# Pooling of batches 1 to 3 in column tiles, its exponentials turned by transposing DMAs, side jobs grouped next to phases, input loads paced by a GpSimd copy

## The chip, the cores and the metric

The kernel runs on one core of a Trainium2 chip. Its engines are PE (TensorE: matmuls; PEld is its weight load), DVE (VectorE), ACT (ScalarE), POOL (GpSimd) and SP (SyncE, which here only issues DMAs). The metric is device microseconds (us) of one execution, as a median over runs; less is better.

## The reference

Four batches of 12544 tokens with 128 features, 32 inducing vectors:

```python
def mab(q, kv):
    s = scale * (q @ kv.transpose(0, 2, 1))
    s = s - s.max(-1, keepdims=True)
    a = np.exp(s)
    a /= a.sum(-1, keepdims=True) + 1e-09
    return a @ kv
h = mab(I, x)          # pooling: 32 vectors h from 12544 tokens
y = mab(x, h)          # every token attends to the 32 vectors
g = np.maximum(y @ w1, y @ w2)
out = g @ w_out        # d_ff = 1024, result f32
```

## The kernel before, in words

A batch is cut into 98 chunks of 128 tokens; there are 392 chunks. The kernel rewrites max(y w1, y w2) w_out as relu(y (w2 - w1)) w_out plus a linear part y w1 w_out, and folds h into the weights: `hwd` = h (w2 - w1) and `m1` = h w1 w_out, so that y itself is never formed.

For each batch there are two parts.

- Pooling. The tokens of a batch arrive as seven loads (`load_x`, L160, issued by POOL) into tiles `xn` (14 chunks each), of which there are 12. SP turns them into `xT` with 14 transposing DMAs (`transpose_x_dma`, L164). For each of the seven parts, `p1_scores` (L244) makes 14 matmuls with a chunk of `xT` as weights (128x128) and the 32 inducing vectors as moving operand, and ACT takes the exponential into `et` (tokens on partitions). `p1_accum` (L262) makes 14 more matmuls with a chunk of `xn` as weights and the 32 columns of `et` as moving operand; the sum stays in PSUM for a part, then DVE adds it to `hacc` (L303). POOL adds up the exponentials themselves in `eacc` (L305), folds them (`small_fold`, L308), and `small_h` sums them over partitions with four f32 matmuls against ones (L339), takes the reciprocal and scales. `small_hwd` and `small_m1` make the folded weights. Batch 0 is pooled before the main loop, in another way; batches 1 to 3 are pooled in the main loop, between the output work of the batch before.
- Output. `stage` (L464) makes the second exponentials `e2` for a block of up to 16 chunks: four matmuls in column tiles (128 rows by 32 columns of the PE array, all four side by side, L479), then one exponential. A `phase` (L771) is up to four jobs in row tiles (32 rows by 128 columns, L827), one per PSUM bank: hidden units of `hwd` for one quarter, or the linear part. A relu of 128x512 on ACT (L843) or DVE (L846) takes each bank to SBUF. `final_one` (L652) is a full-array matmul of 128x128x128, eight per chunk, 3136 in all; when a group of up to four chunks is complete, DVE scales it by the softmax denominator (`evict_group`, L692) into one of six tiles `o` and SP stores it (L717).

The order of instructions on every engine is written by the program itself when it is built: an object `Clock` keeps an estimated time for PE, ACT, DVE and each of the eight PSUM banks, and the loop at L909 picks the next piece of PE work from it. A change of tiling mode (full array, row tiles, column tiles) is charged in that estimate. Pooling jobs are put on a list `jobs_at` by the number of finished output chunks (L859 to L876); `side_work` (L880) takes the first pending job if its inputs are ready by the estimate and the PE is in full-array mode. The estimate knows nothing of SP's queue: a transposed part counts as usable a fixed time after its issue.

Of the kernel before, what the change touches and what calls it, by code (L numbers as in the profile page):

```python
# [16 lines left out]
INF = 1e9  # L17
# [85 lines left out]
def kernel(  # L103
# [53 lines left out]
            xn_at[b, i] = xn_tiles[nslot % NXN]  # L157
            nslot += 1

    def load_x(b, i):  # L160
        k0, n = parts[b][i]
        nc.gpsimd.dma_start(out=xn_at[b, i][:, 0:n, :], in_=xr[b, :, k0 : k0 + n, :])  # L162

    def transpose_x_dma(b, j):  # L164
# [23 lines left out]
    inducingT = consts.tile([C, M], F16, name="inducingT")  # L188
    m1bd = consts.tile([128, 4, C], F16, name="m1bd")
    rep32 = consts.tile([128, 128], F32, name="rep32")  # L190
    diag = consts.tile([128, M], F32, name="diag")

    with tc.manual_schedule(engines={ET.PE, ET.DVE, ET.Activation, ET.Pool, ET.SP}):
        nc.sync.dma_start(ind_sb, inducing)
# [16 lines left out]
        for q in range(4):  # L211
# [1 line left out]
        nc.gpsimd.memset(m1bd, 0.0)  # L213

        nc.vector.reduce_sum(out=diag, in_=identity32.rearrange("p (k m) -> p m k", m=M), axis=AX.X)
        nc.vector.tensor_scalar(
            out=rep32.rearrange("p (k m) -> p k m", m=M),
            in0=diag[:, None, :].broadcast_to((128, 4, M)),
            scalar1=DOWN / scale,
            scalar2=None,  # L220
            op0=ALU.mult,
        )

        st = [dict() for _ in range(B)]

# [36 lines left out]
        def p1_accum(b, i):  # L262
            k0, n = parts[b][i]
            et, ready = st[b].pop(("et", i))
            xn = xn_at[b, i]
            if b == 0:
                last = i == len(parts[0]) - 1
                ck.wait(ready, "p1")
                for j in range(n):
                    nc.tensor.matmul(  # L270
                        out=st[0]["hps"][:, 0:M],
                        lhsT=xn[:, j, :],
                        rhs=et[:, j, :],
                        start=(i == 0 and j == 0),
                        stop=(last and j == n - 1),
                    )
                for j in range(0, n, 4):
                    m = min(4, n - j)
                    nc.tensor.matmul(
                        out=st[0]["eps"][0 : m * M, 0:1],  # L280
                        lhsT=et[:, j : j + m, :].rearrange("p k m -> p (k m)"),
                        rhs=ones16[:, 0:1],
                        start=(i == 0 and j == 0),
                        stop=(last and j + m >= n),
                        skip_group_check=True,
                    )
                st[0]["end"] = ck.run(0.029 * n + 0.03 * ((n + 3) // 4))
                return
            bi, ps = bank([128, 512])
            ck.wait(max(ready, ck.bank[bi]), "p1")  # L290
            for j in range(n):
                nc.tensor.matmul(  # L292
                    out=ps[:, 0:M], lhsT=xn[:, j, :], rhs=et[:, j, :], start=(j == 0), stop=(j == n - 1)
                )
            end = ck.run(0.029 * n)
            if i == 0:
                st[b]["hacc"] = smp.tile([C, M], F32, name=f"hacc_{b}", tag="hacc")
                nc.vector.tensor_copy(out=st[b]["hacc"], in_=ps[:, 0:M])
                st[b]["eacc"] = smp.tile([128, P1, M], F32, name=f"eacc_{b}", tag="eacc")
                nc.gpsimd.tensor_copy(out=st[b]["eacc"], in_=et)  # L300
            else:
                acc = st[b]["hacc"]
                nc.vector.tensor_add(out=acc, in0=ps[:, 0:M], in1=acc)  # L303
                acc = st[b]["eacc"]
                nc.gpsimd.tensor_add(out=acc, in0=acc, in1=et)  # L305
            ck.bank[bi] = ck.on_dve(end, 0.1)

        def small_fold(b):  # L308
            e = st[b]["eacc"]
            nc.gpsimd.tensor_add(out=e[:, 0:7, :], in0=e[:, 0:7, :], in1=e[:, 7:14, :])  # L310
            nc.gpsimd.tensor_add(out=e[:, 0:3, :], in0=e[:, 0:3, :], in1=e[:, 3:6, :])

        def small_h(b):
            hT4 = smp.tile([C, 4, M], F16, name=f"hT4_{b}", tag="hT4")
            if b == 0:


                nc.vector.tensor_scalar(
                    out=hT4,
                    in0=st[0]["hps"][:, None, 0:M].broadcast_to((C, 4, M)),  # L320
                    scalar1=DOWN,
                    scalar2=None,
                    op0=ALU.mult,
                )
                st[b]["hT4r"] = ck.on_dve(st[0]["end"], 0.3)
                ck.bank[st[0]["hb"]] = st[b]["hT4r"]
                es = smp.tile([128, 1], F32, name="es_0", tag="es")
                nc.scalar.copy(out=es, in_=st[0]["eps"][:, 0:1])
                ready = ck.on_act(st[0]["end"], 0.2)
                st[b]["hT4"] = hT4.rearrange("c q m -> c (q m)")  # L330
                return es, ready
            rec = smp.tile([C, M], F32, name=f"hrec_{b}", tag="hrec")
            if True:
                bi, ps = bank([128, 512])
                e = st[b]["eacc"]
                use = [0, 1, 2, 6]
                ck.wait(ck.bank[bi], "p1")
                for n, i in enumerate(use):
                    nc.tensor.matmul(  # L339
                        out=ps[:, 0:M], lhsT=ones32, rhs=e[:, i, :], start=(n == 0), stop=(n == len(use) - 1)  # L340
                    )
                end = ck.run(0.11 * len(use))
                nc.vector.reciprocal(out=rec, in_=ps[:, 0:M])
                ck.bank[bi] = ck.on_dve(end, 0.35)
                hsrc = st[b]["hacc"]
            nc.vector.tensor_mul(
                hT4,
                hsrc[:, None, :].broadcast_to((C, 4, M)),
                rec[:, None, :].broadcast_to((C, 4, M)),
            )  # L350
            st[b]["hT4r"] = ck.on_dve(0.0, 0.25)
            st[b]["hT4"] = hT4.rearrange("c q m -> c (q m)")

        def small_sums(es, ready):
# [239 lines left out]
        state = {"g": 0, "mm": 0, "lin": 0, "done": 0, "issued": 0}  # L594
        ptr = [[0, 0] for _ in range(4)]
        chunks_done = [0]

        def unit_src(g, chunk, jb):
            q, t = chunk
# [82 lines left out]
        def evict_group(g, end):  # L682
# [33 lines left out]
            for b, c, s, m in runs:  # L716
                nc.sync.dma_start(out=outr[b, :, c : c + m, :], in_=osb[:, s : s + m, :])  # L717
            chunks_done[0] += n

        def finals_left():  # L720

# [28 lines left out]
            return g  # L750

        LINEAR_AHEAD = 18
        MARGIN = 0
        LIMIT = -16

        def plan_phase(linear=True):
# [93 lines left out]
                ptr[q][1] += 1  # L850
                state["issued"] += 1

        jobs_at = {}
        DONE0 = [0, 98, 196, 294]

        def at(n, f, *a):
            jobs_at.setdefault(n, []).append((f, a))

        for b in range(1, B):  # L859
            base = DONE0[b - 1]  # L860
            p_first, p_step = (16, 5) if b == 1 else (0, 7)
            t_first, t_step = (8, 2.2) if b == 1 else (-14, 3.4)
            for i in range(7):
                s = int(p_first + p_step * i)
                at(base + s, p1_scores, b, i)
                at(base + s + 2, p1_accum, b, i)
            end = base + int(p_first + p_step * 6)
            at(end + 2, small_fold, b)
            at(end + 4, small_h, b)
            at(end + 5, small_hwd, b)  # L870
            at(end + 6, small_m1, b)
            for j in range(14):
                at(base + int(t_first + t_step * j), transpose_x_dma, b, j)
            if b > 1:
                for i in range(7):
                    at(base - 34 + 3 * i, load_x, b, i)  # L876

        pending = []

        def side_work():  # L880
            while jobs_at and min(jobs_at) <= chunks_done[0]:
                pending.extend(jobs_at.pop(min(jobs_at)))
            while pending:
                f, a = pending[0]
                if f in (p1_scores, p1_accum, small_h, small_hwd, small_m1):
                    if min(ck.bank) > ck.pe + 0.1 or ck.mode != "full":
                        return
                    if f is p1_scores and st[a[0]]["T", 2 * a[1] + 1] + 6.0 > ck.pe:
                        return
                    if f is p1_accum and st[a[0]]["et", a[1]][1] > ck.pe:  # L890
                        return
                    if f is small_m1 and a[0] == 0 and w_of["w1out"] > ck.pe:
                        return
                    if f in (small_hwd, small_m1) and st[a[0]]["hT4r"] > ck.pe:
                        return
                    pending.pop(0)
                    f(*a)
                    return
                pending.pop(0)
                f(*a)  # L900

        phase(plan_phase(False))
        phase(plan_phase(False))
        stage(blocks[1])
        weights_3()
        pending.append((small_m1, (0,)))
        nstage = 2
        START = ck.pe
        while state["g"] < len(groups):  # L909
            side_work()  # L910
            need = [ptr[q][0] for q in range(4)]
            if nstage < len(blocks):
                left = []
                for q in range(4):
                    next_job(q)
                    k, u = ptr[q]
                    left.append(sum(len(blk.units[q]) for blk in blocks[k:nstage] if q < len(blk.units)) - u)
                free = nstage < NE2 or min(g.blk.index for g in groups[state["g"] :]) > nstage - NE2
                if min(left) <= 3 and free and min(ck.bank) <= ck.pe + 0.1 and all(
                    "hT4" in st[qu.b] and "hwd" in st[qu.b] for qu in blocks[nstage].quarters if qu  # L920
                ):
                    stage(blocks[nstage])
                    nstage += 1
                    continue
            jobs = plan_phase()
            tp = INF
            tf = final_ready()
            useful = len(jobs) == 4 or jobs and (tf >= INF or nstage == len(blocks) and lag() <= 48)
            if useful and len(jobs) > 0:
                fr = sorted(ck.bank)[len(jobs) - 1]  # L930
                tp = max([fr - 0.095] + [(a.blk.staged if kind == "L" else a.staged) for kind, q, a, u in jobs])
            if tp < INF and lag() <= 128 + LIMIT and (tp <= ck.pe - MARGIN or tp <= tf and tf > ck.pe):
                phase(jobs)
            elif tf < INF:
                keep_busy(tf)
# [40 lines left out]
```

## Time and profile before

| what | value |
|---|---|
| median of 13 runs | 340.91 us (338.96 to 343.48) |
| the profiled execution | 339.68 us |
| its span | 337.9 us |
| DMA | 50.60 MB, mean 150 GB/s |
| POOL adds of exponentials (L305) | 18 of 1034 ns |
| issue of an input load on POOL (L162) | 550 ns |

The span is the part of the execution between its first and last traced instruction; 1.8 us lie around it. Busy times are unions of the instructions' own intervals, and matmuls overlap their neighbours, so PE's work is better read from the distance between the starts of groups in the timeline than from the length of a matmul: a matmul of 128 columns lasts 220 ns, yet its successor starts 56 ns later.

### The profile page before, as it was taken

Reading aid. Unit: us, or ns where it says so; the run is one execution under the profiler, and the core shown is the slowest. Engines: PE = TensorE matmul, PEld = TensorE weight load, DVE = VectorE, ACT = ScalarE, POOL = GpSimd, SP = SyncE. Lnnn points to the kernel's source line nnn. Section 1 sums busy time; section 2 is a strip of 40 time slices with the busy share of each in tenths; the row PEclk is TensorE's granted clock in tenths of the full one; section 3 lists DMA queues with packets and bytes.
Section 4 is the critical chain, followed back from the end, with each engine's and each line's share of the span. In section 5 each row is a group of like instructions: output and inputs, shape, how many; then the busy total and the mean of one; then the engine's idle time right before and its main releaser. Section 6 shows DMA issues by size and latency. Waiting matters only on the chain.

```text
span 337.9 us, 13042 instructions
## 1 busy us (share of the span) xinstructions
PE 328.9 (97%) x5636; PEld 255.3 (76%) x5636; DVE 286.8 (85%) x525; ACT 279.4 (83%) x532; POOL 45.5 (13%) x72
## 2 busy tenths in 40 slices
PE   7888999999999999999999999999999999999996
PEld 3776767777777777787777778877777777777786
DVE  2248989989988899998899989889999998898873
ACT  2559888986996998888998888887989899989961
POOL 7270002234000012134000012121000000000000
PEclk9999999999999999999999999999999999999999
DMA  7999889938985769529975679631222321231233
GB/s 129 212 263 213 190 205 188 198 109 166 242 228 152 177 146 187 137 95 175 249 212 139 145 165 199 130 99 66 101 89 95 111 95 72 90 124 67 95 126 111
DMA packets 60313, 50.60 MB, mean 150 GB/s; under 512 B 42304, under 2 KB 44768, under 8 KB 60256
## 3 DMA queue, kind: packets, MB, share of 16 engines
q1 hardware_dynamic: 54576, 35.35, 39.6%
q0 software_dynamic: 5680, 14.42, 22.0%
q8 instruction: 44, 0.72, 0.8%
q14 instruction: 13, 0.11, 0.1%
HBM read 27.80 MB, written 25.69 MB: 158 GB/s over the span
## 4 chain that ended last, share of the span: by engine, by line
PE 85%; POOL 1%; ACT 1%; DMA 1%; DVE 1%; issue 1%; SPq 1%; POOLq 0%
PE ps L652 56%; PE ps L827 21%; PE ps L479 2%; PE ps L249 2%; PE ps L292 2%; PE ps L339 1%; DMA xT<-xn 1%; PE ps L519 1%; POOL eacc L305 1%; DVE relu L846 1%; ACT relu L843 1%; POOL eacc L310 0%; SPq L168 0%; PE ps L371 0%; PE ps L630 0%
## 5 line engine op out<-in xcount | busy, mean ns | idle before, releaser
L843 ACT ACTIVATE relu<-ps 128x512 f16<-128x512 f32 x460 | 245.8, 600 | 38.3 <-PE ps L827 32.0
L846 DVE TENSOR_SCALAR relu<-ps 128x512 f16<-128x512 f32 x324 | 208.7, 681 | 21.1 <-PE ps L827 19.0
L652 PE MATMUL ps<-woutp,relu 128*128 128x128 f16 x3136 | 222.3, 220 | 0.0
L652 PEld LDWEIGHTS <-relu 128*128 128x128 f16 x3136 | 177.3, 98 | 38.4 <-issue 27.8
L827 PE MATMUL ps<-e,hwd 32*128 32x512 f16 (+2 forms) x880 | 88.7, 360 | 0.4 <-ACT e L491 0.3
L692 DVE TENSOR_TENSOR o<-ps,rp 128x512 f32<-128x512 f32 (+3 forms) x108 | 68.5, 634 | 8.3 <-PE ps L652 5.4
L827 PEld LDWEIGHTS <-hwd 32*128 32x128 f16 x880 | 24.9, 91 | 20.8 <-issue 1.1
L827 PE MATMUL ps<-m,e 32*128 32x128 f16 x381 | 38.6, 217 | 0.0
L305 POOL TENSOR_TENSOR eacc<-eacc,et 128x448 f32<-128x448 f32 x18 | 18.6, 1034 | 82.1 <-ACT et L258 82.1
L827 PEld LDWEIGHTS <-e 32*128 32x128 f16 x381 | 21.3, 93 | 2.9 <-issue 0.2
L258 ACT ACTIVATE et<-ps 128x448 f16<-128x448 f32 (+2 forms) x29 | 15.6, 538 | 3.1 <-PE ps L249 3.0
L249 PE MATMUL ps<-inducingT,xT 128*128 128x32 f16 x392 | 15.5, 177 | 1.6 <-DMA xT<-xn 0.8
L162 POOL DMA_DIRECT2D xn<-in_x_dram x29 | 15.7, 550 | 2.3 <-POOLq L960 0.8
L249 PEld LDWEIGHTS <-xT 128*128 128x128 f16 x392 | 13.1, 96 | 2.5 <-DMA xT<-xn 1.0
L300 POOL CAST eacc<-et 128x448 f32<-128x448 f16 x3 | 1.7, 556 | 89.9 <-ACT et L258 89.9
L237 DVE COPY xT<-ps 128x1024 f16<-128x1024 f16 (+2 forms) x8 | 5.1, 633 | 9.6 <-PE ps L233 9.6
L240 ACT COPY xT<-ps 128x768 f16<-128x768 f16 (+2 forms) x8 | 5.6, 704 | 8.8 <-PE ps L233 8.8
L491 ACT ACTIVATE e<-ps 128x512 f16<-128x512 f32 (+2 forms) x21 | 11.9, 571 | 0.0
L479 PE MATMUL ps<-xT,hT 128*32 128x512 f16 (+3 forms) x114 | 10.5, 367 | 0.1
L292 PE MATMUL ps<-et,xn 128*128 128x32 f16 x294 | 10.6, 176 | 0.0
L292 PEld LDWEIGHTS <-xn 128*128 128x128 f16 x294 | 9.7, 96 | 0.0
L233 PE MATMUL ps<-identity,xn 128*128 128x128 f16 x98 | 6.8, 220 | 0.7 <-DMA xn<-in_x_dram 0.7
(75 smaller groups left out, 99.8 us busy)
## 6 DMA issues: line engine op xcount, KB each, us to landing
out_dram<-o SPq DMA_DIRECT2D x90, 256.0 KB, 2.4
xn<-in_x_dram POOLq DMA_DIRECT2D x27, 448.0 KB, 11.7
out_dram<-o SPq DMA_DIRECT2D x10, 128.0 KB, 2.1
wf<-in_moe_w_dram POOLq DMA_DIRECT2D x4, 256.0 KB, 12.1
xT<-xn SPq DMA_TRANSPOSE x42, 3.4
out_dram<-o SPq DMA_DIRECT2D x6, 64.0 KB, 1.8
out_dram<-o SPq DMA_DIRECT2D x2, 192.0 KB, 3.3
xn<-in_x_dram POOLq DMA_DIRECT2D x1, 256.0 KB, 13.7
```

The lines of the kernel that those rows point to most:

```text
L162: nc.gpsimd.dma_start(out=xn_at[b, i][:, 0:n, :], in_=xr[b, :, k0 : k0 + n, :])
L249: nc.tensor.matmul(out=ps[:, j * M : (j + 1) * M], lhsT=xT_tiles[b % 2][:, k0 + j, :], rhs=inducingT, start=True, stop=True,)
L258: nc.scalar.activation(out=et[:, 0:n, :], in_=ps[:, 0 : n * M], func=AF.Exp, scale=scale)
L292: nc.tensor.matmul(out=ps[:, 0:M], lhsT=xn[:, j, :], rhs=et[:, j, :], start=(j == 0), stop=(j == n - 1))
L305: nc.gpsimd.tensor_add(out=acc, in0=acc, in1=et)
L479: nc.tensor.matmul(out=ps[32 * q : 32 * (q + 1), 128 * t : 128 * (t + n)], lhsT=hq, rhs=xT[:, c : c + n, :], start=True, stop=True, tile_p ...
L491: nc.scalar.activation(out=blk.e2[:, 0 : 128 * wd], in_=ps[:, 0 : 128 * wd], func=AF.Exp, scale=st[0]["rs"] if blk.b == 0 else scale,)
L652: nc.tensor.matmul(out=g.ps[:, 128 * c : 128 * (c + 1)], lhsT=g.blk.relu[q][:, 128 * (jb * w4 + t) : 128 * (jb * w4 + t + 1)], rhs=woutp[: ...
L692: nc.vector.tensor_mul(osb[:, 0:n, :], g.ps[:, 0 : n * C].rearrange("p (s c) -> p s c", s=n), rp)
L827: nc.tensor.matmul(**seq[i])
L843: nc.scalar.activation(out=dst, in_=src, func=AF.Relu)
L846: nc.vector.tensor_scalar(out=dst, in0=src, scalar1=0.0, scalar2=None, op0=ALU.max)
```

## The change

- In batches 1 to 3 the tokens are pooled in six units of 16 chunks and a rest of two chunks. `pool_scores` makes four matmuls in column tiles with the inducing vectors as weights and 512 tokens each as moving operand, as `stage` does; the exponential `eu` (inducing vector and column tile on partitions) also gives its row sums through the accumulator output. `pool_turn` turns `eu` into `eT` with one transposing DMA on SP (18 in all). `pool_accum` makes 16 matmuls in column tiles with 32 columns of `eT` as weights and a chunk of `xn` as moving operand; DVE adds 128x128 to `hacc`. The rest goes the old way for its scores and joins the last unit.
- `small_rep` and the new `small_h` add up the four column tiles with a constant matrix `repd`: one f32 matmul for the sums, a reciprocal and a scaling on DVE, one f32 matmul for h, and a copy. The adds on POOL, `small_fold` and the four f32 matmuls per batch are gone.
- `pool_scores`, `pool_accum` and `stage` are placed by `column_work`, which is asked when the PE is not in full-array mode and before each phase; `stage` may now go up to five units ahead. `side_work` no longer stops at a job that is not ready.
- The loads of batches 2 and 3 are each preceded on POOL by a copy of one column of the last output tile, at the same place in the job list as before.

```diff
...
-    def load_x(b, i):
+    def load_x(b, i, after=None):
         k0, n = parts[b][i]
+        if after is not None:
+            nc.gpsimd.tensor_copy(out=pace, in_=after[0][:, 0, 0:1])
         nc.gpsimd.dma_start(out=xn_at[b, i][:, 0:n, :], in_=xr[b, :, k0 : k0 + n, :])
...
+        U = 16
+        NU = K // U
+        REST = K - U * NU
...
+        def pool_scores(b, u):
+            if u == 0:
+                st[b]["es"] = smp.tile([128, NU + 1], F32, name=f"es_{b}", tag="esu")
+                nc.gpsimd.memset(st[b]["es"], 0.0)
             bi, ps = bank([128, 512])
-            ck.wait(max(ready, ck.bank[bi]), "p1")
-            for j in range(n):
+            ck.wait(ck.bank[bi], "p1")
+            for g in range(4):
                 nc.tensor.matmul(
-                    out=ps[:, 0:M], lhsT=xn[:, j, :], rhs=et[:, j, :], start=(j == 0), stop=(j == n - 1)
+                    out=ps[32 * g : 32 * (g + 1), :],
+                    lhsT=inducingT,
+                    rhs=xT_tiles[b % 2][:, U * u + 4 * g : U * u + 4 * (g + 1), :],
+                    start=True,
+                    stop=True,
+                    tile_position=(0, 32 * g),
+                    skip_group_check=True,
                 )
-            end = ck.run(0.029 * n)
-            if i == 0:
...
+            end = ck.run(0.226, "col")
+            eu = etp.tile([128, 512], F16, name=f"eu_{b}_{u}", tag="eu", bufs=3)
+            nc.scalar.activation(
+                out=eu, in_=ps, func=AF.Exp, scale=scale, accum_out=st[b]["es"][:, u : u + 1]
+            )
+            ck.bank[bi] = ck.on_act(end, 0.65)
+            st[b]["eu", u] = eu, ck.bank[bi]
+        def pool_rest(b):
+            bi, ps = bank([128, 512])
+            ck.wait(ck.bank[bi], "p1")
+            for j in range(REST):
+                nc.tensor.matmul(
+                    out=ps[:, j * M : (j + 1) * M],
+                    lhsT=xT_tiles[b % 2][:, U * NU + j, :],
+                    rhs=inducingT,
+                    start=True,
+                    stop=True,
+                )
+            end = ck.run(0.029 * REST)
+            et = etp.tile([128, P1, M], F16, name=f"et_{b}", tag="et")
+            nc.scalar.activation(out=et[:, 0:REST, :], in_=ps[:, 0 : REST * M], func=AF.Exp, scale=scale)
+            ck.bank[bi] = ck.on_act(end, 0.2)
...
+            eT = etp.tile([128, 4, 128], F16, name=f"eT_{b}_{u}", tag="eT", bufs=4)
+            nc.sync.dma_start_transpose(eT, st[b]["eu", u][0].rearrange("p (j t) -> p j t", j=4))
+            st[b]["eT", u] = eT, ck.pe
+        def pool_accum(b, u):
+            bi, ps = bank([128, 512])
+            ck.wait(ck.bank[bi], "p1")
+            eT = st[b]["eT", u][0]
+            last = u == NU - 1
+            for j in range(4):
+                for g in range(4):
+                    nc.tensor.matmul(
+                        out=ps[32 * g : 32 * (g + 1), 0:128],
+                        lhsT=eT[:, j, 32 * g : 32 * (g + 1)],
+                        rhs=xn_of(b, U * u + 4 * g + j),
+                        start=(j == 0),
+                        stop=(j == 3 and not (last and g < REST)),
+                        tile_position=(0, 32 * g),
+                        skip_group_check=True,
+                    )
+            if last:
+                et = st[b]["et"][0]
+                for g in range(REST):
+                    for rhs, lo, n in ((xn_of(b, U * NU + g), 0, 128), (ones16[:, 0:1], 128, 1)):
+                        nc.tensor.matmul(
+                            out=ps[32 * g : 32 * (g + 1), lo : lo + n],
+                            lhsT=et[:, g, :],
+                            rhs=rhs,
+                            start=False,
+                            stop=True,
+                            tile_position=(0, 32 * g),
+                            skip_group_check=True,
+                        )
+            end = ck.run(0.26, "col")
+            if u == 0:
+                st[b]["hacc"] = smp.tile([128, C], F32, name=f"hacc_{b}", tag="hacc")
...
-                nc.vector.tensor_add(out=acc, in0=ps[:, 0:M], in1=acc)
-                acc = st[b]["eacc"]
-                nc.gpsimd.tensor_add(out=acc, in0=acc, in1=et)
-            ck.bank[bi] = ck.on_dve(end, 0.1)
-        def small_fold(b):
-            e = st[b]["eacc"]
-            nc.gpsimd.tensor_add(out=e[:, 0:7, :], in0=e[:, 0:7, :], in1=e[:, 7:14, :])
-            nc.gpsimd.tensor_add(out=e[:, 0:3, :], in0=e[:, 0:3, :], in1=e[:, 3:6, :])
+                nc.vector.tensor_add(out=acc, in0=ps[:, 0:128], in1=acc)
+            ck.bank[bi] = ck.on_dve(end, 0.2)
+            if last:
+                es = st[b]["es"]
+                nc.vector.tensor_copy(out=es[0 : 32 * REST, NU : NU + 1], in_=ps[0 : 32 * REST, 128:129])
+                esr = smp.tile([128, 1], F32, name=f"esr_{b}", tag="esr")
+                nc.vector.reduce_sum(out=esr, in_=es, axis=AX.X)
+                st[b]["esr"] = esr
+                ck.bank[bi] = st[b]["esrr"] = ck.on_dve(end, 0.2)
+        def small_rep(b):
+            bi, ps = bank([128, 512])
+            ck.wait(ck.bank[bi], "p1")
+            nc.tensor.matmul(out=ps[:, 0:1], lhsT=repd, rhs=st[b]["esr"], start=True, stop=True)
+            end = ck.run(0.11)
+            rec = smp.tile([128, 1], F32, name=f"rec_{b}", tag="rec")
+            nc.vector.reciprocal(out=rec, in_=ps[:, 0:1])
+            acc = st[b]["hacc"]
+            nc.vector.tensor_scalar(out=acc, in0=acc, scalar1=rec, scalar2=None, op0=ALU.mult)
+            ck.bank[bi] = st[b]["haccr"] = ck.on_dve(end, 0.4)
...
-            rec = smp.tile([C, M], F32, name=f"hrec_{b}", tag="hrec")
-            if True:
...
-                for n, i in enumerate(use):
-                    nc.tensor.matmul(
-                        out=ps[:, 0:M], lhsT=ones32, rhs=e[:, i, :], start=(n == 0), stop=(n == len(use) - 1)
-                    )
...
+            bi, ps = bank([128, 512])
+            ck.wait(ck.bank[bi], "p1")
+            nc.tensor.matmul(out=ps[:, 0:128], lhsT=st[b]["hacc"], rhs=repd, start=True, stop=True)
+            end = ck.run(0.25)
+            nc.vector.tensor_copy(out=hT4.rearrange("c q m -> c (q m)"), in_=ps[:, 0:128])
...
-            p_first, p_step = (16, 5) if b == 1 else (0, 7)
+            p_first, p_step, p_lag = (22, 4.2, 12) if b == 1 else (2, 9, 10)
...
+            for u in range(NU):
+                s = int(p_first + p_step * u)
+                at(base + s, pool_scores, b, u)
+                at(base + s, pool_turn, b, u)
+                at(base + s + p_lag, pool_accum, b, u)
+            at(base + s + 2, pool_rest, b)
+            end = base + s + p_lag
+            at(end, small_rep, b)
+            at(end, small_h, b)
+            at(end, small_hwd, b)
+            at(end, small_m1, b)
             for j in range(14):
                 at(base + int(t_first + t_step * j), transpose_x_dma, b, j)
             if b > 1:
                 for i in range(7):
-                    at(base - 34 + 3 * i, load_x, b, i)
+                    at(base - 34 + 3 * i, load_x, b, i, last_out)
...
+        def ready(f, a):
+            d = st[a[0]]
+            now = ck.pe
+            if f is pool_scores:
+                return d.get(("T", (U * a[1] + U - 1) // (P1 // 2)), INF) + 8.0 <= now
+            if f is pool_rest:
+                return d.get(("T", 13), INF) + 6.0 <= now
...
+            if f is pool_accum:
+                return d.get(("eT", a[1]), (0, INF))[1] + 8.0 <= now and (a[1] < NU - 1 or "et" in d)
...
+        def column_work(banks):
+            if sorted(ck.bank)[banks - 1] > ck.pe + 0.12:
+                return False
+            if want_stage(5):
+                stage(blocks[state["stage"]])
+                state["stage"] += 1
+                return True
+            jobs = [job for job in pending if job[0] in COL and ready(*job)]
+            late = jobs and chunks_done[0] >= due[jobs[0]] + 6
+            if jobs and (ck.mode == "col" or len(jobs) > 1 or late):
+                pending.remove(jobs[0])
+                f, a = jobs[0]
+                f(*a)
+                return True
+            return False
...
+        def want_stage(ahead):
...
+            return min(left) <= ahead and free and all(
...
+            if ck.mode != "full" and column_work(1):
+                continue
+            if min(ck.bank) <= ck.pe + 0.1 and want_stage(1):
+                stage(blocks[state["stage"]])
+                state["stage"] += 1
+                continue
...
-            if tp < INF and lag() <= 128 + LIMIT and (tp <= ck.pe - MARGIN or tp <= tf and tf > ck.pe):
+            early = 0.2 if ck.mode == "col" else 0.0
+            if tp < INF and lag() <= 128 + LIMIT and (tp <= ck.pe + early or tp <= tf and tf > ck.pe):
+                if column_work(len(jobs) + 1):
+                    continue
                 phase(jobs)
...
```

## The prediction

> **What bounds the kernel now.** First the page: busy shares, then the chain that ended last.
>
> ```profile
> span 337.9 us, 13042 instructions
> PE 328.9 (97%) x5636; PEld 255.3 (76%) x5636; DVE 286.8 (85%) x525; ACT 279.4 (83%) x532; POOL 45.5 (13%) x72
> PE 85%; POOL 1%; ACT 1%; DMA 1%; DVE 1%; issue 1%; SPq 1%; POOLq 0%
> ```
>
> PE is 97% busy and 85% of the chain. A busy PE need not be a full one, so next the timeline, where the distance between starts is what a group costs.
>
> ```profile
> 71.28 0.40 PE L827 MATMUL ps<-e,hwd 32*128 32x512 f16 x4
> 71.61 0.40 PE L479 MATMUL ps<-xT,hT 128*32 128x512 f16 x4
> 71.94 0.34 PE L652 MATMUL ps<-woutp,relu 128*128 128x128 f16 x3
> 72.12 0.50 PE L292 MATMUL ps<-et,xn 128*128 128x32 f16 x14
> 72.47 0.22 PE L652 MATMUL ps<-woutp,relu 128*128 128x128 f16 x1
> 72.53 0.50 PE L249 MATMUL ps<-inducingT,xT 128*128 128x32 f16 x14
> 72.88 0.77 PE L652 MATMUL ps<-woutp,relu 128*128 128x128 f16 x11
> 73.58 0.40 PE L827 MATMUL ps<-e,hwd 32*128 32x512 f16 x4
> ```
>
> No start is late: three final matmuls take 0.18 us (72.12 less 71.94), 56 ns each; a phase, and a stage in column tiles, take 0.33 with a change of mode in each; a pooling part of 14 takes 0.35. Eleven finals at 56 ns are 0.61, and the phase after them starts 0.70 later, so a change of mode costs about 0.10, and a bare phase or stage 0.23. PE is full here: time is what PE is given to do. Last, who could take over:
>
> ```profile
> 45.00:240.00 195.00, 193.63 (x3408) 150.90 (x3405) 176.26 (x321) 169.04 (x325) 30.90 (x41) 1.00 0.73 165
> L168 SPq DMA_TRANSPOSE xT<-xn x42: 1220/1275/2566, 41.8 to 217.6; - x42
> DMA to landing us min/median/max: 2.9/3.4/4.8
> ```
>
> In the stretch with all the pooling (us; then PE, PEld, DVE, ACT, POOL busy) DVE has 90%, ACT 87%. A transposing DMA of seven chunks holds SP's queue 1.28 us and lands 3.4 us after its issue.
>
> **What PE loses.** In batches 1 to 3: 21 score parts and 21 accumulating parts, 42 x 0.35 = 14.8 us. The f32 sums over partitions:
>
> ```profile
> 75.83 0.22 PE L652 MATMUL ps<-woutp,relu 128*128 128x128 f16 x1
> 76.23 1.08 PE L339 MATMUL ps<-eacc,ones 128*128 128x32 f32 x8 [0.18 <-POOL eacc L311]
> 77.14 0.56 PE L652 MATMUL ps<-woutp,relu 128*128 128x128 f16 x7
> ```
>
> 0.91 us of work, and 0.34 of waiting ahead of it (76.23 less 75.83, less one final): three times, 2.7 and 1.0. Removed work 17.5 us.
>
> **What PE gains.** Counted in the compiled order of the changed kernel: 18 `pool_scores` of four matmuls, the shape of the 71.61 row, 0.23 each: 4.1. 18 `pool_accum` of 16 matmuls in column tiles, 128 columns moving. Only one place shows two sets of 128 columns or more back to back in column tiles:
>
> ```profile
> 247.52 0.46 PE L479 MATMUL ps<-xT,hT 128*32 128x128 f16 x8
> 247.91 0.90 PE L652 MATMUL ps<-woutp,relu 128*128 128x128 f16 x13
> ```
>
> This is a set of four matmuls of 128 columns and then one of four of 512 (two stages): 0.39 in all, less 0.23 for the second and 0.10 for the mode leaves 0.06 for four matmuls of 128 columns. Four such sets are 0.24; I take 0.25. Bounds: four times 56 ns, 0.22, if the tiles hide each other wholly; 16 times the 25 ns a pooling matmul takes (0.35 over 14), 0.40, if each is issued as a narrow full-array matmul is. So 4.5 us, 4.0 to 7.2. The rest of two chunks: 6 score matmuls, 12 accumulating ones, 0.3. `small_rep`: an f32 matmul of one column, 0.23 (0.91 over four): 0.7. The new `small_h` is f32 with 128 columns moving, which no row shows: from 0.23 (the weights decide, as at 32 columns) to 0.91 (the columns do); I take 0.45, the geometric middle, since neither end is nearer: 1.4 for three, between 0.7 and 2.7. Sum 11.0.
>
> The Trainium skill has a rule against `pool_accum`: "TensorE: Matmul & The Clock Gate", Part 3, under the mechanism, says that a weight load overlaps matmuls in flight only where the row group differs, and column tiles all share their rows; its weight-load section puts 32 columns at 27 ns. By an estimate from that page each set would pay four loads, 0.16 instead of 0.06, so 0.65 a unit and 7 us over the 18, which would eat the whole gain. The row disagrees: the second set of the 247.52 group starts 0.06 after the first.
>
> **Changes of mode.** Grouping side jobs at phases sounds like fewer. Counted over the main loop, the order has 470 before and 478 after: `pool_scores` and `pool_accum` now need a mode of their own, and find one in use only in part (41 runs of column work against 26). 8 x 0.10 = 0.8 us lost. The 222 phases and 3136 finals are the same, as are the 27 stages in cost.
>
> **Waits that go and come.** Gone: 1.0 ahead of the sums, and 1.0 where the first scores of batch 1 waited for `xT` (the page: L249, DMA xT<-xn 0.8, and the weight load with it); batch 1 starts six chunks later. Come, first: batch 1's scores leave the opening of the loop, so relus move up into it, where ACT and DVE are overloaded already (in the first 8 us of PE work the order gives DVE 10.7 us, before 9.0, counted at 0.60 a relu, the distance of relus back to back on DVE in the trace). I charge 0.9. Second: `small_rep`, `small_h` and `small_hwd` each follow a DVE step with 0.8 to 1.9 us of finals between; matmul end, DVE queue and the step (0.17 to 0.29 by the rows of L362 and L346) come to about 1.1, so 0.3 a batch, 0.9. Third: `eT`. In the order 9.7 to 14.5 us of PE work lie between a unit's scores and its accumulation; needed are 0.23, an exponential of 0.61 (L491), up to 0.6 of queue and 3.4 of landing, 4.9. Walking SP's queue through the order as well (1.3 a turn or transpose, 0.45 a store, each store after its group), the cover left in batches 2 and 3 is 2.4 to 9 us. In batch 1 three score units come in a row while SP still issues batch 1's own transposes; before, 14 of these and 8 stores filled SP from 41.8 to 67.9 without a pause worth the name. The third turn stands behind two transposes, two turns and a store, some 6.5 us, then lands 3.4 later: just as PE comes for it. I charge 0.5. `pool_turn` also holds output stores behind it on SP; with six `o` tiles and stores that land in 2.3 us none is short. The pacing copy and its load stand alone on POOL now; the copy reads an `o` tile for about 0.1 us (the smallest POOL rows), and tiles for the loads are free well before (what they overwrite is due at least 40 chunks earlier). Nothing charged.
>
> The sum: -17.5 + 11.0 + 0.8 = -5.7; waits -2.0 + 2.3; **-5.4 us**. A few of the planner's filler matmuls (21 to 13, 0.4) go too: **-5.8**. Against the profiled execution, 339.7, that is 333.9; that one stood 1.2 below the median 340.9, so **335.1** for the median.
>
> **Can ACT and DVE follow?** The order moves 11 relus from DVE to ACT. ACT in 45 to 240: 169 less 21 x 0.55 plus 18 x 0.61 plus three small ones plus 11 x 0.53 (245.8 over 460) makes 175; DVE 176 less 7 for relus, plus about 3 for wider adds and the small chain, 172. The stretch shrinks to 189, so 93% and 91%. Nobody is full, yet there is less air than at 87 and 90. No row shows an exponential with an accumulator output; it costs nothing more, or at most one more tiny ACT instruction (L328, 0.16): 3 us of ACT over 18, 94%.
>
> **Rivals.**
> (1) *Relu engines bind.* If ACT and DVE can't be kept over 90% busy in bursts, the stretch needs 347/2/0.90 = 193 instead of 189 and gives 4 us back: 339. For: 88% is the most they have shown on the mean, and the opening is already theirs. Against: PE never waited for them from 45 on. 0.16.
> (2) *The turn is late* (the slower side). Place: PE before `pool_accum`. Price: with landings at 8 us instead of 3.4 (input loads take 11.7), each unit with less than 4.6 of cover stalls for the difference: 5 in batch 1, 7 in the others, 12 in all, 347. It decides from landings of about 7 us on, where the stalls equal the 5.8 won. For: all cover in batch 1 is gone. Against: transposes stayed within 4.8 with loads in flight. 0.13.
> (3) *Column weights cost* the upper bound, 0.40 a unit: +2.7, 337.8. 0.06.
> (4) *It doesn't do what it says*: the column work finds idle PE that I count as full, or none of the new waits comes: 332. 0.09.
> Forecast 0.56, its own range 332.5 to 338.
>
> **How the numbers follow.** A measurement of this kernel tells about 0.5% from no change, so faster is under 339.2 and slower over 342.6. Faster: 0.56 + 0.09 + 0.06 + half of (1) = 0.79, less some of the forecast's tail, 0.76. Same: the other half of (1) and that tail, 0.11. Slower: (2), 0.13. The unknown prices at their lower ends (`pool_accum` -0.5, `small_h` -0.7, no new waits -2.3) give 331.6, and (4) goes slightly under; at their upper ends (+2.7, +1.3) 339.1, with what (1) may add 341.5. Range 331 to 341.5.
>
> **What would show it.** Right: `pool_accum` starts 0.25 apart from its successor without a mode change; PE without gaps after 45 us; ACT near 93%. Wrong: PE waiting for eT<-eu (2), finals waiting for relus (1), `pool_accum` at 0.4 or more (3).

## The result and the profile after

| | before | changed |
|---|---|---|
| median, us | 340.84 | 346.28 |
| runs | 48 (338.96 to 344.12) | 11 (342.97 to 352.93) |
| ratio of the two | | 1.0133, 95% interval 1.010 to 1.0165 |
| span of the profiled execution, us | 337.9 | 344.7 |

The changed kernel is 1.3% slower, where 1.7% faster was forecast. Ratios here and below leave disturbed runs out (those far above the quickest of the same kernel), so for a kernel whose own time scatters the ratio can stand lower than its median says.

The page of the changed kernel, the same three lines as before the change:

```profile
span 344.7 us, 12617 instructions
PE 328.1 (95%) x5406; PEld 247.3 (72%) x5406; DVE 281.7 (82%) x521; ACT 284.2 (82%) x561; POOL 24.8 (7%) x62
PE 82%; DMA 4%; SPq 1%; ACT 1%; DVE 1%; issue 0%; DVEq 0%
```

PE has 230 matmuls fewer and nearly the same busy time, on a longer span; DMA is 4% of the chain instead of 1%. The stretch with the pooling, as a window of the changed kernel (columns: us, PE, PEld, DVE, ACT, POOL busy, granted clock, DMA share, GB/s):

```profile
45.00:240.00 195.00, 186.97 (x3097) 139.91 (x3095) 166.48 (x303) 167.48 (x340) 10.06 (x30) 0.97 0.84 174
```

PE was idle for 8 us here, before 1.4, and the clock is 0.97, before 1.00. The timeline of PE shows where (start, us, line, group, and in brackets the idle time and who ended it). In batch 1:

```profile
66.82 0.38 PE L911 MATMUL ps<-e,hwd 32*128 32x512 f16 x1
...
69.48 0.39 PE L911 MATMUL ps<-e,hwd 32*128 32x512 f16 x2 [2.28 <-ACT eu L325]
...
70.52 0.45 PE L736 MATMUL ps<-woutp,relu 128*128 128x128 f16 x5
72.88 0.24 PE L336 MATMUL ps<-inducingT,xT 128*128 128x32 f16 x2 [1.90 <-DMA xT<-xn]
72.95 1.55 PE L736 MATMUL ps<-woutp,relu 128*128 128x128 f16 x13
```

and later, in batches 2 and 3:

```profile
122.74 0.39 PE L314 MATMUL ps<-xT,inducingT 128*32 128x512 f16 x1
123.85 0.39 PE L314 MATMUL ps<-xT,inducingT 128*32 128x512 f16 x2 [0.72 <-DMA xT<-xn]
125.43 0.38 PE L314 MATMUL ps<-xT,inducingT 128*32 128x512 f16 x1 [1.19 <-DMA xT<-xn]
...
223.02 0.40 PE L361 MATMUL ps<-xn,eT 128*32 128x128 f16 x16
223.25 0.39 PE L314 MATMUL ps<-xT,inducingT 128*32 128x512 f16 x4
225.24 0.41 PE L361 MATMUL ps<-xn,eT 128*32 128x128 f16 x16 [1.60 <-DMA eT<-eu]
```

These five waits are 7.7 us. All end with a transposing DMA: the first by way of ACT, whose fourth exponential of batch 1 could not overwrite the first `eu` before its turn had landed, with the relus queued behind it:

```profile
ACT eu L325 <- DMA eT<-eu: 4.8, 2, 3.0
```

(the waits of the changed kernel between 60 and 76 us: 4.8 us in all, 2 times, 3.0 the longest). Then the clock, windows of the same kernel, columns as above:

```profile
71.50:78.30 6.80, 5.42 (x87) 3.94 (x88) 2.27 (x6) 3.13 (x9) 0.00 (x0) 0.50 0.59 136
78.30:85.00 6.70, 6.70 (x120) 5.09 (x118) 6.40 (x11) 6.42 (x13) 0.00 (x0) 1.00 0.31 100
126.00:129.50 3.50, 3.50 (x37) 2.65 (x34) 1.55 (x3) 1.18 (x3) 0.00 (x0) 0.51 1.04 244
```

After the waits PE runs at half its clock for 6.8 us, and for 3.4 us after those of batch 2. Half of what it was busy there, (5.4 + 3.5)/2, is 4.5 us lost. Waits and clock together are 12.2 us. The best check of this sum is the last run below (h2_l32_b34_eu3), the same PE work with no wait of PE over 0.5 us after 45 us and no half clock: its span is 331.1 us, 13.6 less than the changed kernel's, so 12.2 of 13.6 are named. (Against the kernel before, the span grew by 6.8; 12.2 less the 5.8 forecast comes near it, but the 5.8 already holds 2.3 charged for new waits.)

Why the transposes were late is read on SP. Batch 1 in the changed kernel, from the timeline of SP's queue:

```profile
63.61 2.62 SPq L171 DMA_TRANSPOSE xT<-xn  x2
66.33 1.22 SPq L351 DMA_TRANSPOSE eT<-eu  x1
67.64 0.53 SPq L801 DMA_DIRECT2D out_dram<-o  x1
68.22 1.26 SPq L171 DMA_TRANSPOSE xT<-xn  x1
69.58 3.51 SPq L351 DMA_TRANSPOSE eT<-eu  x2
```

The first three exponentials ran on ACT from 59.9 to 61.6; their turns are issued at 66.3, 69.6 and 70.9, behind batch 1's own transposes, and the last of those at 68.2 behind a turn. Batch 2:

```profile
107.27 3.76 SPq L171 DMA_TRANSPOSE xT<-xn  x1
111.14 0.53 SPq L801 DMA_DIRECT2D out_dram<-o  x1
112.12 5.51 SPq L171 DMA_TRANSPOSE xT<-xn  x1
```

Two issues of 3.8 and 5.5 us instead of 1.3. They did not wait for their own tokens: both read the first load of batch 2, issued 13.7 us before the first of them, and these loads landed within 12.2 us. Landings of `xT<-xn` reach 13.6 us (before at most 4.8). POOL issued the paced loads of batch 2 between 93.6 and 107.9 us; before the change they had gone out between 76.3 and 79.7, as soon as POOL was done with its adds.

### The profile page after: what moved, and what is told of

It reads as the page before. It is cut to its first block, busy times and chain, and to the rows that moved or that the text cites. A ratio compares the mean times of both kernels' runs of the same rounds, so it can differ in the third digit from the quotient of the medians.

```text
span 344.7 us, 12617 instructions
## 1 busy us (share of the span) xinstructions
PE 328.1 (95%) x5406; PEld 247.3 (72%) x5406; DVE 281.7 (82%) x521; ACT 284.2 (82%) x561; POOL 24.8 (7%) x62
## 4 chain that ended last, share of the span: by engine, by line
PE 82%; DMA 4%; SPq 1%; ACT 1%; DVE 1%; issue 0%; DVEq 0%
PE ps L736 55%; PE ps L911 20%; DMA xT<-xn 3%; PE ps L562 2%; PE ps L361 2%; ACT relu L927 1%; DMA eT<-eu 1%; PE ps L314 1%; SPq L171 1%; PE ps L602 1%; DVE relu L930 1%; SPq L801 0%; PE ps L454 0%; SPq L351 0%; PE ps L402 0%
## 5 line engine op out<-in xcount | busy, mean ns | idle before, releaser
L927 ACT ACTIVATE relu<-ps 128x512 f16<-128x512 f32 x471 | 249.3, 604 | 33.0 <-PE ps L911 25.0
L930 DVE TENSOR_SCALAR relu<-ps 128x512 f16<-128x512 f32 x313 | 201.8, 681 | 31.2 <-PE ps L911 28.0
L736 PE MATMUL ps<-woutp,relu 128*128 128x128 f16 x3136 | 219.9, 221 | 0.1
L325 ACT ACTIVATE eu<-ps 128x512 f16<-128x512 f32 x18 | 10.9, 617 | 6.6 <-DMA eT<-eu 4.8
L164 POOL COPY pace<-o 128x1 f32<-128x1 f32 x14 | 2.6, 186 | 147.9 <-DVE o L776 144.3
L314 PE MATMUL ps<-xT,inducingT 128*32 128x512 f16 x72 | 8.0, 396 | 1.9 <-DMA xT<-xn 1.9
L361 PE MATMUL ps<-xn,eT 128*32 128x128 f16 x288 | 7.4, 236 | 1.6 <-DMA eT<-eu 1.6
L361 PEld LDWEIGHTS <-eT 128*32 128x32 f16 x288 | 5.0, 104 | 4.6 <-issue 2.1
L612 DVE RECIPROCAL rp<-ps 128x16 f32<-128x16 f32 (+2 forms) x28 | 6.6, 237 | 0.0
L602 PE MATMUL ps<-ones_q,e 128*128 128x4 f16 x102 | 6.6, 166 | 0.0
```

The costliest lines, as they stand in the source:

```text
L314: nc.tensor.matmul(out=ps[32 * g : 32 * (g + 1), :], lhsT=inducingT, rhs=xT_tiles[b % 2][:, U * u + 4 * g : U * u + 4 * (g + 1), :], start ...
L325: nc.scalar.activation(out=eu, in_=ps, func=AF.Exp, scale=scale, accum_out=st[b]["es"][:, u : u + 1])
L361: nc.tensor.matmul(out=ps[32 * g : 32 * (g + 1), 0:128], lhsT=eT[:, j, 32 * g : 32 * (g + 1)], rhs=xn_of(b, U * u + 4 * g + j), start=(j = ...
L602: nc.tensor.matmul(out=ps[:, 4 * t : 4 * t + 4], lhsT=blk.e2[:, 128 * t : 128 * (t + 1)], rhs=ones_q, start=True, stop=True,)
L736: nc.tensor.matmul(out=g.ps[:, 128 * c : 128 * (c + 1)], lhsT=g.blk.relu[q][:, 128 * (jb * w4 + t) : 128 * (jb * w4 + t + 1)], rhs=woutp[: ...
L927: nc.scalar.activation(out=dst, in_=src, func=AF.Relu)
```

## The experiments

Two theories grew out of this. L: a transposing DMA beside input loads in flight is slow, and the pacing put the two side by side. Q: in batch 1 SP's one queue holds 14 transposes, and the turns on top of them are late. S is the rival to L: SP is overfull anyhow; E the rival to Q: three `eu` buffers are too few. A further rival is that column work as such costs what it wins. In the table, "loads together" keeps the pacing copies: the seven loads are due at one place instead of spread over 18 chunks.

| run | what differs from the changed kernel | median, us | ratio to before (95%) |
|---|---|---|---|
| e1_nopace | no pacing copies | 349.61 | 1.0228 (1.016 to 1.030) |
| e2_early | paced loads due 22 chunks earlier | 361.21 | 1.0569 (1.049 to 1.065) |
| e3_eu6 | six `eu` buffers | 346.75 | 1.0122 (1.007 to 1.017) |
| e6_before_pace | kernel before, with pacing copies | 355.82 | 1.0424 (1.035 to 1.050) |
| f1_burst | loads together, 40 chunks ahead | 341.66 | 1.0018 (0.999 to 1.004) |
| f2_burst_eu6 | the same, six buffers | 341.10 | 0.9995 (0.995 to 1.004) |
| f4_burst_l32 | f1 and batch 1 ten chunks later | 354.26 | 1.0399 (1.036 to 1.044) |
| f3_burst_eu6_l32 | f2 and batch 1 ten chunks later | 353.84 | 1.0401 (1.034 to 1.046) |
| g1_l32_b34 | loads together, 34 ahead; six buffers; batch 1 ten later | 334.19 | 0.9787 (0.974 to 0.983) |
| g2_l28_b40 | loads together, 40 ahead; six buffers; batch 1 six later | 337.04 | 0.9855 (0.980 to 0.991) |
| h1_l32_paced | g1 with the paced loads | 343.23 | 0.9933 (0.988 to 0.999) |
| h2_l32_b34_eu3 | g1 with three buffers | 333.50 | 0.9777 (0.972 to 0.983) |

**The pacing alone, in the kernel before.**

```diff
+        if after is not None:
+            nc.gpsimd.tensor_copy(out=pace, in_=after[0][:, 0, 0:1])
...
-                    at(base - 34 + 3 * i, load_x, b, i)
+                    at(base - 34 + 3 * i, load_x, b, i, last_out)
```

> The kernel before with the pacing copies alone added to its loads. Theory L: the loads of batches 2 and 3 go out some 20 us later, beside the first transposes, which then take 3 to 5 us on SP and make p1_scores of batch 2 or 3 wait: 2 to 6 us slower than before, 343 to 347. Rival S: the pacing does nothing here, since SP has no turns to issue: within 1 us of 340.8.

Slower by 4.2%, 14 us, far over the 2 to 6 expected. SP of this run, and PE at the same place:

```profile
106.09 6.59 SPq L170 DMA_TRANSPOSE xT<-xn  x1
```

```profile
115.24 0.34 PE L252 MATMUL ps<-inducingT,xT 128*128 128x32 f16 x7 [4.35 <-DMA xT<-xn]
116.56 0.37 PE L252 MATMUL ps<-inducingT,xT 128*128 128x32 f16 x7 [0.98 <-DMA xT<-xn]
```

There are no turns in this kernel, so S falls: the pacing alone makes transposes late. The trace has such waits in batch 3 too, 2.70 and 2.83 us near 200 us, and PE runs at half clock for some 6.8 us behind each pair, so more is lost than in the changed kernel. Why the old scores wait longer wasn't tried.

**Loads elsewhere.**

```diff
-                    at(base - 34 + 3 * i, load_x, b, i, last_out)
+                    at(base - 34 + 3 * i, load_x, b, i)
```

> The changed kernel without the pacing copies: the loads of batches 2 and 3 go out as soon as their tiles are free. Theory L (the pacing put the loads of batches 2 and 3 beside the first transposes of those batches, whose issue on SP then took 3.8 and 5.5 us): the two waits of pool_scores at 123 us (1.1 and 1.6 us in the changed kernel's trace) and the 3.4 us of half clock at 126 us are gone, 2.7 + 1.7 = about 4 us less, 342 us; the waits near 67 and 71 us stay. Rival S (SP's queue alone is overfull, whatever the loads do): the waits at 123 us stay and the time is within 1 us of 346. With the loads of batch 2 out at about 27 us they could also collide with batch 1's transposes, which would show as longer issues on SP between 42 and 66 us.

A miss: 349.6. The waits near 123 us were gone, as L had it, but five loads of batch 2 now went out between 26 and 35 us and met batch 1's first transposes, one of which took 4.6 us to issue; the wait for ACT at 67 us, now at 72, grew from 2.7 to 3.7 us between starts. That is not the whole loss: in this trace the clock of the first 45 us is 0.85, against 1.00, and the first transpose goes out at 45.7 us instead of 41.8. No run tells whether the early loads have a part in that.

```diff
-                    at(base - 34 + 3 * i, load_x, b, i, last_out)
+                    at(base - 56 + 3 * i, load_x, b, i, last_out)
```

> The changed kernel with the paced loads of batches 2 and 3 due 22 output chunks (some 17 us) earlier, pacing kept. Theory L: the loads have landed before the first transpose of the batch, the transposes take 1.3 us on SP again and the waits of pool_scores at 123 us go with the half clock after them: about 4 us less, 342 us. Rival S: no change, 346 us, and the transposes of batch 2 still wait.

A miss again, and the worst: the first load of batch 2, at 65.2 us, met batch 1's turns, and PE waited 6.82 us for ACT; those of batch 3, issued from 154.9 to 167.3, met batch 2's, two of which landed only 22.2 and 23.3 us after their issue. PE in this run:

```profile
183.80 0.62 PE L361 MATMUL ps<-xn,eT 128*32 128x128 f16 x16 [14.09 <-DMA eT<-eu]
```

Both misses fit L in its general form: wherever the loads fall beside transposing DMAs, those are late. With the turns there are few places left: after the last turn of one batch and before the first transpose of the next.

```diff
-                    at(base - 34 + 3 * i, load_x, b, i, last_out)
+                    at(base - 40, load_x, b, i, last_out)
```

> The changed kernel with the seven loads of a batch due together, 40 output chunks before that batch's output begins: after the last turn of the pooling before, and some 20 us before the first transpose of the batch, which is where the kernel before had them by its POOL queue. Theory L (a transposing DMA that runs beside input loads is slow, whichever of the two was moved): the issue of the first transposes is back at 1.3 to 2.2 us, the waits of pool_scores near 123 us and the half clock behind them go (4 us), the wait for eT at 223 us may stay: 342. Rival S (SP overfull): 346, with the waits where they were.

341.66, as L had it: 3.9 us less than the changed kernel by the two ratios. The copies are still there, so it is the time of the loads that counts and not the copies. The wait for `eT` at 223 us went too. The loads go out from 89.2 to 93.1 us, the first transpose of batch 2 takes 1.3 us again, and from 100 us on PE is full at full clock, while batch 1's waits stand as they were:

```profile
45.00:100.00 55.00, 50.76 (x822) 37.30 (x822) 45.10 (x84) 43.52 (x90) 4.75 (x15) 0.94 0.84 167
100.00:240.00 140.00, 139.92 (x2365) 105.76 (x2362) 126.89 (x228) 129.68 (x262) 4.89 (x15) 1.00 0.84 182
```

**Buffers.**

```diff
-            eu = etp.tile([128, 512], F16, name=f"eu_{b}_{u}", tag="eu", bufs=3)
+            eu = etp.tile([128, 512], F16, name=f"eu_{b}_{u}", tag="eu", bufs=6)
```

> The changed kernel with six eu buffers instead of three. Theory E (the fourth exponential of batch 1 holds ACT until the first turn has landed, 3 us, and the relus behind it hold PE for 2.7 us at 67 us): ACT waits for eT<-eu nowhere, the 2.7 us wait of the phase goes, 1.8 us of ACT's second wait too; but the last transposes of batch 1 land no earlier, so pool_rest at 71 us then waits longer, by up to the 2.7 us won. So between 343.5 (nothing handed on) and 346 (all handed on to pool_rest). Rival (SP alone decides when batch 1 is through): 346, with the whole wait at pool_rest.

346.75, no gain. The wait for ACT (2.28) is gone, and the next in line has grown by nearly as much, from 1.90 to 3.80:

```profile
73.05 0.24 PE L336 MATMUL ps<-inducingT,xT 128*128 128x32 f16 x2 [3.80 <-DMA xT<-xn]
```

> The same with six eu buffers. With Theory L giving 342, the ACT wait of 3 us at 66 us goes as in the run with six buffers alone, where pool_rest then waited 4.0 us instead of 2.1: 341 to 342, since the last transpose of batch 1 lands no earlier. If batch 1's waits were the buffers' alone: 338.

341.10 against 341.66: the same, and PE waits at `pool_rest` for 4.5 us. The buffers only choose who waits.

**Batch 1 later.**

```diff
-            p_first, p_step, p_lag = (22, 4.2, 12) if b == 1 else (2, 9, 10)
+            p_first, p_step, p_lag = (32, 4.2, 12) if b == 1 else (2, 9, 10)
```

> The loads together, three eu buffers, and batch 1's pooling due ten output chunks later, so that its turns follow batch 1's transposes on SP instead of standing between them. Theory Q (the waits at 67 and 71 us are SP's queue, filled by batch 1's 14 transposes, with the turns of 1.2 us each on top): both waits and the half clock behind them (4.8 us of waiting, 3.4 of clock) go: 342 less 8 = 334 to 336, under the kernel before by the 5.8 us of PE work that was forecast. Rival (three buffers are too few at any time): the wait of ACT for eT<-eu stays, 339 to 342.

> All three: loads together, six eu buffers, batch 1's pooling ten chunks later. Theories L and Q together: no wait of PE over 0.5 us after 45 us but perhaps the one at 223 us, no half clock before the end, 333 to 336. If column work as such costs (modes, banks, the accumulator's extra ACT instruction), there are no long waits and it is still 339 or more.

Neither tells of Q. With batch 1 later and the loads 40 chunks ahead, two loads of batch 2 stand in the program before the pooling of the batch 1 tiles that they overwrite, so that part of batch 1 is pooled from batch 2's tokens, and PE waited 20 and 18 us for that load at 78 us. The loads were then set six chunks later (34 ahead), past that pooling:

> The changed kernel with batch 1's pooling due ten output chunks later, six eu buffers, and each batch's seven loads together, 34 output chunks before its output (six later than in the run with loads together alone, so that every tile they overwrite has been pooled). Theories L (transposes beside loads) and Q (batch 1's transposes and turns in one SP queue) together: no PE wait over 1 us after 45 us, no half clock between 45 us and the end, and the 5.8 us of PE work are won: 333 to 337. If column work as such costs (modes, banks, the extra accumulator instruction on ACT), there are no long waits and it is still 339 or more. If the loads at 34 chunks reach the first transposes, waits near 105 us and 340 or more.

> The same with batch 1's pooling only six chunks later (one turn then still stands before the last transpose of batch 1 on SP) and the loads together 40 chunks ahead. Theory Q: the waits at 67 to 72 us shrink from 4.7 us to under 2, and the half clock with them if no wait is long: 334 to 338.

334.19 and 337.04, both as expected. The stretch with the pooling in the first:

```profile
45.00:240.00 195.00, 194.96 (x3334) 147.13 (x3331) 178.57 (x328) 178.44 (x362) 9.67 (x30) 1.00 0.85 180
```

PE is full at full clock, with DVE and ACT at 92%: column work as such shows no cost beyond its slots. With batch 1 only six chunks later, two waits for `eT` of 1.08 and 0.88 us remain near 74 us; the profiled execution of that run also had its opening, up to 45 us, at 0.89 of the clock (1.00 in the changed kernel, 0.96 in the run at 334.19), at a place that these edits don't touch, so not all of its 3 us are Q's.

**Each cause alone.**

> The changed kernel with batch 1's pooling ten chunks later and six eu buffers, but the loads paced as in the changed kernel. Theory L: batch 1 is free of waits as in the run at 334.2, and the loads beside the first transposes of batches 2 and 3 bring the waits near 105 to 125 us back: 334.2 plus the 4 us that the loads together were worth, 338; some 3 us of long PE waits after 100 us in the trace. Rival (once SP has air in batch 1, the pacing is harmless): 334 to 335.

The paced loads bring the loss back: ratio 0.9933 against 0.9787, 5 us, and the median 343.23 lies 9 us higher, with runs from 336.7 to 347.8. The same run gives batch 1 alone: it differs from e3_eu6 only in `p_first`, and 0.9933 against 1.0122 is 6.4 us. In its trace a transpose takes 4.64 us to issue at 113.5, and PE waits for `xT` at 122:

```profile
113.48 4.64 SPq L171 DMA_TRANSPOSE xT<-xn  x1
```

```profile
122.34 0.38 PE L314 MATMUL ps<-xT,inducingT 128*32 128x512 f16 x1 [1.64 <-DMA xT<-xn]
```

> The run at 334.2 with three eu buffers, as in the changed kernel. Theory Q (the turns were late because SP was full, and the buffers only passed that on to ACT): with the turns in time three buffers are enough, 334 to 335. Rival E (three buffers are too few whenever three units stand in a row): ACT waits for eT<-eu, 336 or more.

333.50: three buffers are enough here, so E falls. But SP has no more air than in the changed kernel. Its queue in this run:

```profile
64.59 1.26 SPq L171 DMA_TRANSPOSE xT<-xn  x1
65.94 1.22 SPq L351 DMA_TRANSPOSE eT<-eu  x1
67.25 2.00 SPq L801 DMA_DIRECT2D out_dram<-o  x1
69.31 1.27 SPq L171 DMA_TRANSPOSE xT<-xn  x1
70.67 1.01 SPq L801 DMA_DIRECT2D out_dram<-o  x2
71.78 2.54 SPq L351 DMA_TRANSPOSE eT<-eu  x2
```

The first turn still goes out at 66 us, 5.6 us after its exponential, and still stands before the last transpose. What changed is who asks when: only one exponential runs before 66 us instead of three, the fourth at 72.0, when the first turn has landed (it was due before 66 us in the changed kernel), and `pool_rest` at 76.1, after the last transpose. So Q holds in one half: the waits of batch 1 come from SP's queue, mostly its 14 transposes. That turns on top of them make it overfull isn't shown; one turn of 1.2 us stood before the last transpose with and without the waits.

This is the quickest version, 2.2% under the kernel before, and differs from the changed kernel only in the two edits to `p_first` and to the place of the loads.

## Why the prediction was wrong, point by point

- *PE's work: right.* The changed kernel's order has `pool_accum` and the next column job 0.23 us apart (223.02 and 223.25), against 0.25 taken; the weights of column tiles overlap, as the row of two stages said and the rule weighed against it did not. `small_h` took 0.28 from its start to the next group, against 0.45 taken, `small_rep` 0.21 against 0.23. Where PE waits for nothing, the change wins 2.1 to 2.2%, some 7.5 us, against 5.8 forecast: `small_h` was cheaper by 0.5 in three, and of the 2.3 us charged for new waits few came.
- *"Nothing charged" for the pacing: the first step that failed.* It looked at the copy, at POOL and at when tiles are free, and not at when the transfers would run. The job list names the same place for the loads before and after, but POOL used to reach that place when its adds were done; the copy ties it to the output, 17 to 32 us later, where the transposes of the next batch begin. Worth 3.9 us in the changed kernel (f1 against it), 14 us in the kernel before.
- *"I charge 0.5" for the turns of batch 1: the second.* The walk through SP's queue had the right mechanism and was short: it put the third turn some 6.5 us back, and it went out 9.3 us after its exponential (61.6 to 70.9). But the graver fault is that it named `pool_accum` alone as the one who waits. Two others stood nearer: ACT's next exponential, which needs the buffer that the turn reads, with relus queued behind it; and the last transpose of `xT`, at the end of the same queue, with `pool_rest` waiting for it. Between f2 and g1 this is 2.1%, 7.1 us, between e3 and h1 6.4: 4.2 of waits in the changed kernel's trace, and the clock. The two steps together, 3.9 and 7.1, are 11.0 of the 12.1 us that lie between the ratios of the changed kernel and of the quickest version.
- *The clock was no term at all.* 10.2 us at half clock, some 4.5 us lost, took the price of the waits from 7.7 to 12.2.
- *The rivals.* The one on the slower side, late turns, had the mechanism (a blocked SP queue) and a fitting size, but its place, `pool_accum`, was that of only 1.6 us, and landings of turns stayed at 2.3 to 4.2 us; that its 347 lies near the 346.28 measured is luck. It got 0.13 because transposes had "stayed within 4.8 with loads in flight"; in the trace before, loads and transposes of batches 2 and 3 hardly met. ACT and DVE did not bind: at 92% PE waits for nothing. The extra ACT instruction of an accumulator output exists, 0.2 us long; the three exponentials in a row at 60 us start 0.57 apart.

## What to carry to other kernels

Ask of a moved transfer not only whether it is in time, but what will be in flight beside it: work taken off an idle engine's queue can be what kept two transfers apart. A late DMA is priced by everyone who waits for it, the writer that wants its source buffer back included; here more buffers only passed the wait on to the next who asked. A late DMA is free when nobody asks for it yet: the quickest version won by asking later, with the queue as it was. When PE is bound, the sum of its slots tells what can be won; whether it is won is decided by the longest queue that the slots depend on.

## What the runs showed of the hardware

- The issue of a transposing DMA on SP takes 1.22 us for four chunks and 1.28 for seven: nearly a fixed price, though without such loads single ones took up to 2.7. Beside input loads in flight the slowest took 3.8 to 6.6 us, and landings reached 13.6 in the changed kernel, instead of at most 4.8 before. In the quickest version too, batch 2's first two took 2.55 and 3.70 and landed after up to 9.9 us, and PE didn't wait for them. Why they are slow there, no run shows.
- Half clock can follow short waits: 2.28 and 1.90 us of idle PE within 6 us came before 6.8 us of half clock, and 0.72 and 1.19 us before 3.4. The Trainium skill, "TensorE: Matmul & The Clock Gate", in the table "Why this matters for your kernels", warns of idle gaps over some 3 us; here two shorter gaps close together were enough, and in e3_eu6 a single one of 2.56 us (3.4 us of half clock followed). But it doesn't always follow: not after 1.60 us at 225 us, not after 2.11 us in h1, and not after 1.08 and 0.88 us within 4 us in g2. The runs give no threshold.
- In two kernels with paced loads PE stood still with nothing to wait for that the profile shows, in one of them just while a transpose was stuck in its issue on SP (113.48 above; PE from 113.8 to 115.9):

```profile
115.92 0.22 PE L736 MATMUL ps<-woutp,relu 128*128 128x128 f16 x1 [2.11 <-issue]
```

What held PE there, no run shows.
